# Softmax attention with bit-built exponentials: one of VectorE's three shifted copies is made by DMA instead

## The chip, the cores and the metric

One core of one Trainium2 chip. The metric is the device time of one execution in microseconds (us). Each kernel was run several times; the text quotes the median. An execution is called slow when it lies over 1.5% above the fastest of the same kernel; such executions are left out of every ratio, though not of the medians.

## The reference

Two independent attention layers over 2048 positions with 32 heads of 16 channels, whose outputs stand side by side.

```python
# A: softmax attention
scores = einsum("bhqd,bhkd->bhqk", q, k) * scale
p = softmax(scores)
o = einsum("bhqk,bhkd->bhqd", p, v)
a = o.reshape(B, S, D) @ wo
# B: linear attention with softmax features
phi_q = concat([softmax(q @ w_phi), softmax(-q @ w_phi)])     # phi_k likewise
kv = einsum("bhsf,bhsd->bhfd", phi_k, v); z = phi_k.sum(s)
b = ((phi_q @ kv) / (phi_q @ z + 1e-6)) @ wo
out = concat([a, b])                                           # along the channels
```

What matters is A: 32 x 2048 x 2048 exponentials. B is small and is woven in between.

## The kernel before

The work of A is cut into 32 units (four heads, 512 query positions) of 16 key tiles. A key tile is 128 keys; its exponentials for the four heads are 128 x 2048 numbers. Most key tiles go to ScalarE, which exponentiates scores out of the score buffers. For up to five of the 16 (`DK`) VectorE builds the exponential from its bits: the score times a constant plus a constant, written as a 16-bit integer, is the bit pattern of a 16-bit float near the exponential. To make the error small, the same bits are used four times, shifted by 0, 256, 512 and 768, and the four results are added by TensorE with weighted values (`VJ`). So a tile costs VectorE four evictions of scores (128 x 512 each, read out of the buffer into which TensorE wrote them) and three copies with an added constant (128 x 2048 each):

```python
# four evictions write the bits into rg[i]; the product with the values follows
firsts.append(put(dv_a, _Task("dve", 0.6, one("dve", cv), [qk], ...)))
put(pe_pd, pv_task(u, firsts + [v_ready[kt]], ..., lambda r: tile(q0.res["i"], r), ...))
for j in range(1, _NPH):                                       # _NPH = 4: three copies
    ad = put(dv_ad, _Task("dve", 0.59, one("dve", lambda e, t, j=j: e.tensor_scalar(
        rg[:, t.res["j"].idx, :], rg[:, q0.res["i"].idx, :], float(sh[j]), 32767.0, ALU.add, ALU.min)),
        firsts, lat=DL, need=[("j", rj_sl, 1, 1)], rel=[lambda: [q0.res["i"]]], port=True))
    put(pe_pd, pv_task(u, [ad, vj_ready[(kt, j)]], ..., lambda r, ad=ad: tile(ad.res["j"], r), ...))
# ... (cut)
```

`put` does not issue anything. A planner in the kernel's source gives each task a duration and a latency (`_Task(engine, us, ..., lat=...)`), simulates the engines, and fixes once the order in which each engine gets its instructions. On the chip every engine then works in that order and waits where a semaphore is not there yet. Whatever comes later than the planner assumed holds up all that stands behind it (in the change TensorE's matmuls wait so for an accumulate 32 times, 57.4 us in all).

## Time and profile before

| | before |
|---|---|
| median of 3 runs | 770.23 us (770.06 to 772.56) |
| span of the profiled run, granted clock | 767.3 us, 0.996 |
| ScalarE busy | 745.1 us, 97% |
| TensorE, VectorE, GpSimd busy | 714.4, 724.6, 149.8 us |
| DMA queues | 23.38 MB |
| wide exponentials' idle time ahead of them | 3.8 us |

Busy time is the sum of an engine's instructions. "Idle before" a group is time in which its engine did nothing until one of its instructions could start, with what ended most of it. The granted clock is TensorE's, as a share of full speed. The lines themselves stand in the prediction below.

### The profile page before, as it was taken

The page shows a single profiled execution, that of the slowest core. Times are in us where ns is not written, and L with a number is a line of the kernel's source. Part 1 is how long each engine was busy: PE and PEld are TensorE (multiplying, and loading weights), DVE is VectorE, ACT ScalarE, POOL GpSimd, SP SyncE. Part 2 cuts the span into 40 slices and gives each one's busy share as a digit, 9 for nine tenths or more (in the row PEclk, how much of TensorE's full clock was granted, in tenths as well). Part 3 has the DMA queues.
Part 4 walks back from the last instruction along what each step waited for, and adds up shares of the span by engine and source line. Part 5 has one row for each costly group of instructions (what it writes and reads, how often), then busy time and mean ns, then how long its engine had stood idle before and what let it go on. Part 6 is the DMA issues. An engine that isn't in the chain of part 4 may idle for free.

```text
span 767.3 us, 17162 instructions
## 1 busy us (share of the span) xinstructions
PE 714.4 (93%) x7122; PEld 217.4 (28%) x7209; DVE 724.6 (94%) x1315; ACT 745.1 (97%) x846; POOL 149.8 (20%) x218
## 2 busy tenths in 40 slices
PE   8999999999899998999899999999999999999996
PEld 3322222223222222232222223322222222222222
DVE  2799999999899999999999999999999999999996
ACT  6999999999899999999999999999999999999994
POOL 3321111110111131212121113222222113121120
PEclk9999999999999999999999999999999999999999
DMA  6200000018300110000000010000000001010002
GB/s 153 68 3 26 8 15 19 16 25 143 97 15 11 33 32 15 8 14 19 16 17 18 16 33 17 16 13 22 26 23 23 26 25 30 18 31 30 11 25 65
DMA packets 43871, 23.38 MB, mean 30 GB/s; under 512 B 31180, under 2 KB 39820, under 8 KB 43788
## 3 DMA queue, kind: packets, MB, share of 16 engines
q1 hardware_dynamic: 42204, 21.45, 10.4%
q8 instruction: 57, 0.93, 0.5%
q10 hardware_dynamic: 1584, 0.79, 0.4%
q14 instruction: 26, 0.21, 0.1%
HBM read 11.81 MB, written 4.45 MB: 21 GB/s over the span
## 4 chain that ended last, share of the span: by engine, by line
ACT 85%; PE 7%; DVE 4%; DMA 2%; issue 0%; SPq 0%; ACTq 0%
ACT pT L962 80%; PE PS L755 2%; DVE rg L1020 2%; PE PS L748 2%; ACT e_k L1172 2%; DMA sums<-X 2%; ACT eT L1235 1%; DVE rg L1031 1%; DMA OT<-in_A_x_dram 1%; ACT Wf L1235 1%; PE PS L877 0%; ACT KT L677 0%; ACT VP L657 0%; DVE Wf L1157 0%; PE PS L646 0%
## 5 line engine op out<-in xcount | busy, mean ns | idle before, releaser
L962 ACT ACTIVATE pT<-PS 128x1024 bf16<-128x1024 f32 (+1 forms) x755 | 706.9, 1093 | 4.0 <-PE PS L748 3.7
L1020 DVE TENSOR_SCALAR rg<-PS 128x512 uint16<-128x512 f32 x524 | 339.7, 682 | 10.5 <-PE PS L748 8.7
L748 PE MATMUL PS<-QT,KT 32*128 32x512 bf16 x2048 | 317.5, 385 | 20.7 <-ACT pT L962 13.8
L1031 DVE TENSOR_SCALAR rg<-rg 128x2048 uint16<-128x2048 uint16 x393 | 256.9, 689 | 0.7 <-PE PS L755 0.5
L748 PEld LDWEIGHTS PS<-QT,KT 32*128 32x128 bf16 x2048 | 80.5, 91 | 284.4 <-ACT pT L962 225.6
L755 PE MATMUL PS<-pT,VP 128*32 128x512 bf16 x1524 | 150.3, 389 | 4.1 <-ACT pT L962 2.0
L755 PE MATMUL PS<-rg,VJ 128*32 128x512 f16 x1572 | 144.0, 386 | 3.6 <-DVE rg L1031 3.1
L755 PEld LDWEIGHTS PS<-pT,VP 128*32 128x32 bf16 x1524 | 39.1, 94 | 82.6 <-issue 51.2
L1182 POOL TENSOR_TENSOR w<-e_k,stat 128x512 bf16<-128x512 bf16 x32 | 33.1, 1056 | 119.5 <-DVE stat L1178 67.3
L755 PEld LDWEIGHTS PS<-rg,VJ 128*32 128x32 bf16 x1572 | 38.3, 95 | 53.9 <-issue 22.3
L755 PE MATMUL PS<-rg,VP 128*32 128x512 f16 x524 | 51.9, 386 | 0.1
L1282 POOL TENSOR_TENSOR w<-w,den 128x256 bf16<-128x256 f32 x32 | 19.3, 619 | 113.4 <-DVE den L1278 70.3
L835 POOL TENSOR_TENSOR OT<-X,Yd 128x256 bf16<-128x256 f32 x30 | 21.7, 741 | 95.8 <-DMA Yd<-scr 78.2
L835 POOL TENSOR_TENSOR Oo<-X,Yd 128x256 bf16<-128x256 f32 x30 | 21.4, 733 | 81.5 <-DMA Yd<-scr 38.1
L649 PE MATMUL PS<-xT,w 128*128 128x512 bf16 x105 | 32.3, 382 | 3.9 <-issue 2.5
L1272 POOL TENSOR_TENSOR w<-w 128x272 f32<-128x272 f32 x32 | 23.7, 760 | 61.1 <-DVE rg L1031 42.8
L1258 DVE TENSOR_TENSOR w<-PS,stat 128x408 f32<-128x408 f32 (+1 forms) x48 | 25.2, 526 | 0.2
L803 DVE COPY X<-PS 128x512 f32<-128x512 f32 x32 | 21.9, 684 | 2.5 <-PE PS L755 2.5
L782 PE MATMUL PS<-ones_t,zer 128*32 128x512 bf16 x252 | 24.2, 388 | 0.0
L685 POOL TENSOR_SCALAR KT<-KT,hmask 128x512 bf16<-128x512 bf16 x12 | 8.3, 692 | 68.7 <-DVE KT L659 46.4
L1175 DVE TENSOR_REDUCE stat<-e_k 128x64 f32<-128x1024 bf16 x16 | 19.4, 1212 | 0.2
L755 PEld LDWEIGHTS PS<-rg,VP 128*32 128x32 bf16 x524 | 13.7, 95 | 19.2 <-issue 10.5
(103 smaller groups left out, 418.4 us busy)
## 6 DMA issues: line engine op xcount, KB each, us to landing
Yd<-scr SPq DMA_DIRECT2D x31, 256.0 KB
out_dram<-e_k SPq DMA_DIRECT2D x16, 128.0 KB, 1.7
out_dram<-OA SPq DMA_DIRECT2D x12, 128.0 KB, 1.7
OT<-Oo SPq DMA_DIRECT2D x60, 16.0 KB, 1.8
w<-in_A_wqkv_dram SPq DMA_DIRECT2D x2, 384.0 KB, 4.9
OT<-in_A_x_dram SPq DMA_DIRECT2D x1, 512.0 KB, 4.7
w<-in_A_wqkv_dram ACTq DMA_DIRECT2D x1, 512.0 KB, 6.4
WOp<-in_A_wo_dram SPq DMA_DIRECT2D x1, 512.0 KB, 6.0
```

Source lines behind the costliest of these rows:

```text
L649: return e.matmul(bank_of(t), w[:, ct, c0:c0 + 128], xT[:, ct, c * 512:(c + 1) * 512], start=(ct == 0), stop=(ct == 3))
L748: return e.matmul(out_ap, KT[32 * r:32 * r + n, g, kt * 128:(kt + 1) * 128], QT[32 * r:32 * r + n, c, g // 2, :], start=True, stop=True, t ...
L755: return e.matmul(PS[32 * r:32 * r + 32, pvb[u].idx, :], lhs(8 * (g // 2) + 2 * r + g % 2), rhs(r), start=t.res["first"], stop=t.res["last ...
L782: P.op("pe", lambda e, r=r: e.matmul(PS[32 * r:32 * r + 32, pvb[u].idx, :], zer[:], ones_t[:].unsqueeze(1).broadcast_to([128, 4, 128]), st ...
L803: xv = _Task("dve", 0.61, one("dve", lambda e, t: e.tensor_copy(X[:, t.res["x"].idx, :], PS[:, pvb[u].idx, :])), [], lat=DL, need=[("x", x ...
L835: ms.append(put(po_n, _Task("pool", 0.7, one("pool", lambda e, t, cs=cs: e.tensor_tensor(OT[:, c % 2, g // 2, cs] if even else Oo[:, ms[0] ...
L962: return e.activation(pT[:, p:p + n, :].rearrange("p a n -> p (a n)"), PS[:, b:b + n, :].rearrange("p a n -> p (a n)"), ACT.Exp, scale=0.25)
L1020: return e.tensor_scalar(rg[:, q0.res["i"].idx, 512 * r:512 * r + 512], PS[:, qk.res["D"].idx, :], ya, yb, ALU.mult, ALU.add)
L1031: ad = put(dv_ad, _Task("dve", 0.59, one("dve", lambda e, t, j=j: e.tensor_scalar(rg[:, t.res["j"].idx, :], rg[:, q0.res["i"].idx, :], flo ...
L1182: ph.append(put(po_phi, _Task("pool", 1.03, one("pool", lambda e, t, a=a: e.tensor_tensor(pk[ph[0].res["k"].idx][:, 512 * a:512 * a + 512] ...
L1258: muls.append(put(dv_y, _Task("dve", 0.485, one("dve", lambda e, t, yv=yv, lo=lo, n=n: e.tensor_tensor(ysv[r0.res["y"].idx][:, 136 * lo:13 ...
L1272: ad = [put(po_y, _Task("pool", 0.73, one("pool", lambda e, t, k=k: e.tensor_tensor(y3(0)[:, 2 * k:2 * k + 2], y3(0)[:, 2 * k:2 * k + 2], ...
```

## The change

The intent is to take work from VectorE, so that it can build more tiles and ScalarE fewer. The first of the three shifted copies is made by two transfers: a constant from DRAM is copied into the buffer (512 KB, issued from SyncE), then GpSimd issues a DMA that adds the bits onto it.

```diff
-    NPT = 15
-    NB, NJ = 2, 4
-    NR = NB + NJ
+    NPT = 13
+    NB, NJ, ND = 3, 2, 3            # buffers: bits, VectorE's copies, DMA's copies
+    NR = NB + NJ + ND
...
-        for j in range(1, _NPH):
+        pf = put(sp_pf, _Task("sp", 0.5, dma(..., lambda e, t, i: e.dma_start(
+            rg[:, t.res["j"].idx, :], sh_d[:].broadcast_to([128, 2048]))), [l_sh], lat=3.3, need=[("j", rd_sl, 1, 1)]))
+        ac = put(po_a, _Task("pool", 1.1, sw(..., lambda e, t: e.dma_start(
+            rg[:, pf.res["j"].idx, :], rg[:, q0.res["i"].idx, :], accum_op=ALU.add)), [pf] + firsts, lat=5.0,
+            rel=[lambda: [q0.res["i"]]]))
+        put(pe_pd, pv_task(u, [ac, vj_ready[(kt, 1)]], ..., lambda r: tile(pf.res["j"], r), ...))
+        for j in range(2, _NPH):
             ad = put(dv_ad, ...
...
-    Oo = sb("Oo", [128, 2, 512], BF)
+    Oo = sb("Oo", [128, 1, 512], BF)
-    OA = sb("OA", [128, 2, 512], BF)
+    OA = sb("OA", [128, 1, 512], BF)
```

Cut from it: a new table of the planner's weights; a start with smaller transposes and a first projection by quarters; key maskings and half of a reduction moved to GpSimd; an ending in which 16 output products stand ahead of the last unit's sum and that sum is copied in halves; sorted final waits; loads of weights moved from ScalarE's queue to SyncE's, and another buffer (`eT`) halved. The planner's two figures: it assumes 3.3 us for the constant and 5.0 us for the accumulate.

## The prediction

> **What bounds the kernel now.** I read the page's busy row first, then the chain of work that ended last, then the groups by shape, and last a table of stretches.
>
> ```profile
> PE 714.4 (93%) x7122; PEld 217.4 (28%) x7209; DVE 724.6 (94%) x1315; ACT 745.1 (97%) x846; POOL 149.8 (20%) x218
> ...
> ACT 85%; PE 7%; DVE 4%; DMA 2%; issue 0%; SPq 0%; ACTq 0%
> ```
>
> Three engines are above 90%, so the busy row alone does not name a bound. The chain does: 85% of it is ScalarE, and four fifths of the span is one line, the exponentials. VectorE, the engine that the change relieves, has 4% of it.
>
> ```profile
> L962 ACT ACTIVATE pT<-PS 128x1024 bf16<-128x1024 f32 x741 | 690.1, 1086 | 3.8 <-PE PS L748 3.5
> L1020 DVE TENSOR_SCALAR rg<-PS 128x512 uint16<-128x512 f32 x524 | 339.7, 682 | 10.5 <-PE PS L748 8.7
> L1031 DVE TENSOR_SCALAR rg<-rg 128x2048 uint16<-128x2048 uint16 x393 | 256.9, 689 | 0.7 <-PE PS L755 0.5
> L962 ACT ACTIVATE pT<-PS 128x1536 bf16<-128x1536 f32 x14 | 21.0, 1503 | 0.2 <-PE PS L748 0.2
> ```
>
> The wide exponentials lost 3.8 us to waiting before them in the whole run. The 393 copies of L1031 are the three shifts of each of 131 VectorE tiles (524 evictions, four to a tile). Their mean of 689 ns is not their cost: they start about 0.6 us apart (the chain shows them at 0.60), so the group takes 257 us rather than 271. The exponentials likewise: 48 in a row in the chain took 44.00 us, 0.917 us each.
>
> ```profile
> 0.00:10.18 10.18, 7.71 (x44) 3.51 (x44) 2.46 (x4) 3.40 (x5) 4.16 (x15) 1.00 0.82 204
> ...
> 40.00:183.00 143.00, 138.20 (x1298) 38.36 (x1309) 141.81 (x246) 143.00 (x155) 18.31 (x26) 1.00 0.10 22
> 183.00:203.00 20.00, 17.28 (x177) 5.64 (x173) 16.88 (x30) 16.71 (x18) 1.00 (x1) 0.91 0.78 169
> ...
> 289.00:640.00 351.00, 327.52 (x3477) 101.64 (x3518) 343.03 (x632) 351.00 (x404) 75.83 (x104) 1.00 0.06 20
> ...
> 755.00:768.00 13.00, 5.92 (x27) 2.72 (x25) 6.02 (x22) 2.64 (x7) 0.00 (x0) 0.89 0.19 57
> ```
>
> Columns: stretch, length, busy time of PE, weight loads, VectorE, ScalarE, GpSimd, granted clock, DMA share, GB/s. From 40 to 183 and from 289 to 640 ScalarE is busy for every microsecond. It idles in three places: the start (first exponential at 10.18), the end (after the last exponential at 754.3), and 3.3 us in 183 to 203, where the loads of the second half hold the DMA engines at 0.78. So the time is ScalarE's work plus those gaps. A faster VectorE shortens nothing by itself; it helps only if ScalarE is given fewer tiles or if a gap shrinks.
>
> [...] its 512 KB loads land in 4.3 to 4.7 us, though among other loads. [...] The copies here do 2048 elements in 689 ns, about 3 a nanosecond, against 0.75 for an eviction (512 in 682 ns)[...].
>
> **The change part by part.** Counts are from the built order of instructions of both kernels.
>
> 1. VectorE's tiles go from 131 to 136 (524 to 544 evictions), its copies from 393 to 272. At 0.6 us, 121 copies fewer take away 73 us and 20 evictions more add 12. The key reduction over 1024 elements (1212 ns, 16 times) becomes a sum of halves on GpSimd and a smaller reduction, perhaps 0.6 us less each, 10 us in all. Twelve key maskings leave for GpSimd, and some evictions come over from ScalarE. VectorE falls by 65 to 70 us, to some 655. None of this is on the chain.
>
> 2. ScalarE, the part that counts. Exponentials go from 741 of two pieces and 14 of three to 716 and 24. A two-piece one takes 0.917; a three-piece one I put at 1503 - (1086 - 917) = 1334 ns. Before: 741 x 0.917 + 14 x 1.334 = 698.2. After: 716 x 0.917 + 24 x 1.334 = 688.6. That is 9.6 us less. Four value evictions (0.49) and three key evictions (about 0.62) fewer are 3.8 us more. ScalarE's work between first and last exponential falls by 13.4 us. This is the main gain, and note how small it is beside 73 us: only five tiles change engine.
>
> 3. TensorE: the five tiles need 3 x 5 x 4 = 60 extra value matmuls, at four in parallel and about 0.216 us, 3 us[...]. It stays at about 714 of a shorter span, some 95%.
>
> 4. GpSimd: [...]32 additions of halves (perhaps 0.7 us), 12 maskings: 30 us of counted work, some 180 in all.
>
> 5. DMA: per tile 512 KB of a constant and 512 KB accumulated. 136 x 1 MB is about 143 MB against 23.38 MB now; the DMA row should go from 10% to half or more.
>
> 6. Start: smaller transposes and a projection by quarters. Chaining the measured pieces (input landed 5.6; transpose 0.3, copy 0.4, four in a pipeline to 7.4; last projection 7.9; eviction 8.7; scores and exponential) I put the first exponential at 9.3 instead of 10.18: 0.9 us.
>
> 7. End: before, 754.83 to 760.41 passes between the last sum's copy and the first output eviction, 3.45 of it 16 output matmuls in a row. Those move ahead of the last sum, which is copied in halves; the final waits are sorted. I take 2.5 us.
>
> Sum without new waits: 770.2 - 13.4 - 0.9 - 2.5 = 753.4.
>
> **The wait that could take the gain back.** TensorE runs in order, so a late accumulated copy stops it, and ScalarE, with two score buffers, soon after. From the built program I counted the exponentials whose scores TensorE issues between a tile's last score matmul and the matmul that waits for its accumulated copy. The median is 9 exponentials, 9 x 0.917 = 8.3 us; the lowest tenth is 7, 6.4 us. Into it must fit matmul (0.4), eviction with a turn in the queue (0.7 to 1.3), GpSimd's issue[...], and the accumulate. [...] So some tiles of the 136 should be late by a fraction of a microsecond to one. As accumulates overlap, I charge 2 us, and 2 us more for the load burst, where 0.78 of the DMA engines is already taken. That gives 757.
>
> **The rivals.**
>
> A. *Late copies become the bound.* If an accumulate takes 7 to 8 us in company, the chain is late at nearly every tile. One microsecond at 136 tiles, with one and a half in flight, is about 90 us. For it: three buffers only, a tile each 5.5 us, each buffer held through constant, accumulate and matmul; the small sums<-X transfer took 4.77 us in the burst. Against: the order was laid out anew, with more distance than the old copies needed. Outcome 785 or more.
>
> B. *The offload relieves an idle resource.* VectorE is not on the chain, and if ScalarE's reduction is eaten by DMA contention in the burst and by the 95% TensorE, only start and end remain: 762 to 768.
>
> C. *Everything is hidden*, and VectorE's slack also removes the small waits of 4 to 5 us in the middle. Then 749 to 752.
>
> D. *TensorE becomes the bound*: the 93% rises to 95%, and each ordering loss goes to the end. It would look like B.
>
> **Range and chances.** The sum without waits lies at 753.4, the 2% line at 770.23 x 0.98 = 754.8. The waits I charge put the middle past that line, and their tail goes one way. Range 748 to 773. Faster by over 2%: 0.38; within 2%: 0.53; slower by over 2%: 0.09, which is rival A.
>
> **What would show it.** Right: ScalarE still over 95% busy and over 80% of the chain, the wide exponentials near 690 us in all, VectorE near 87%, DMA share over half, and waits of TensorE for the accumulated tile under 5 us. Wrong: a row in the waits in which value matmuls wait for the DMA with tens of microseconds, or exponentials with idle time before them well over 4 us (A); ScalarE's idle grown just in 183 to 203 or beside TensorE at 97% (B, D); first exponential not before 9.5, or more than 11 us from last exponential to end, would void parts 6 and 7.

## More of the kernel before

At the end of each unit a chain of small transfers (8 KB for `sums`, 8 KB for `scr`, 256 KB for `Yd`) makes the divisor of the softmax:

```python
d1 = put(sp_q, ... e.dma_start(sums[:, 16 * u:16 * u + 16], X[16 - g % 2:128:32, xi, :]))    # 16 numbers a row
rc = put(dv_n, ... e.reciprocal(rin[...], sums[:, 16 * u:16 * u + 16]), [d1])                # VectorE
d2 = put(sp_q, ... e.dma_start(scr[u]..., rin[...]), [rc])                                   # to DRAM
d3 = put(sp_q, ... e.dma_start(Yd[...], scr[u].unsqueeze(1).broadcast_to([4, 32, 512])), [d2])
ms.append(put(po_n, ... e.tensor_tensor(OT[...], X[...], Yd[...], ALU.mult), [d3]))          # GpSimd
# ... (cut)
```

One more view of this kernel matters later, its longest waits for small transfers: engine and line, then total us, times, longest.

```profile
POOL OT L835 <- DMA Yd<-scr: 78.2, 10, 20.4
...
POOL Oo L835 <- DMA Yd<-scr: 38.1, 7, 10.7
...
DVE rin L817 <- DMA sums<-X: 3.7, 3, 2.4
```

GpSimd stands 116.3 us waiting for `Yd`, and nothing comes of it: nothing urgent is behind it in its queue.

## The result, and the profile after

| | before | after |
|---|---|---|
| median | 770.39 us | 944.2 us (932.78 to 947.09, 4 runs) |
| span of the profiled run, clock | 767.3, 0.996 | 942.8, 0.869 |
| ScalarE busy | 745.1 | 749.9 |
| VectorE, TensorE, GpSimd busy | 724.6, 714.4, 149.8 | 690.0, 788.4, 312.7 |
| DMA | 23.38 MB | 166.05 MB |

The ratio is 1.220 (95% interval 1.209 to 1.231). Ratios here are the mean time of one kernel's fast runs over that of the other's of the same rounds, so they are not quite the ratio of the medians quoted.

The page of the kernel after: busy row, clock and DMA by slices of a fortieth of the span (tenths), the chain of work that ended last.

```profile
PE 788.4 (84%) x7172; PEld 220.1 (23%) x7251; DVE 690.0 (73%) x1214; ACT 749.9 (80%) x821; POOL 312.7 (33%) x399
...
PEclk9997899889798979778969989799987896799699
DMA  6777787879776856877767887877664885869563
...
DMA 37%; PE 28%; DVE 16%; issue 6%; ACT 6%; POOL 3%; SPq 3%; POOLq 0%; DVEq 0%
DMA rg<-rg 17%; PE PS L778 12%; PE PS L771 10%; DVE rg L1061 7%; DMA sums<-X 7%; ACT pT L1003 6%; DMA Yd<-scr 5%; DVE rg L1079 4%; DMA scr<-rin 4%; SPq L596 2%; DMA out_dram<-OA 2%; DMA rg<-sh_d 2%; POOL OT L869 1%; DVE X L831 1%; PE PS L1249 1%
```

No engine is above 84%: where the time went is waiting, not work. The chain has turned over. Before, ScalarE held 85% of it; now it has 6%, and transfers have 37%: the accumulate (`rg<-rg`) 17%, and the three small transfers together 16% (sums 7, Yd 5, scr 4). The clock row is the second surprise: before, the stretches in the prediction show 1.00 nearly everywhere; now 19 of the 40 slices are below nine tenths.

The groups, and the landing of the two new transfers:

```profile
L1003 ACT ACTIVATE pT<-PS 128x1024 bf16<-128x1024 f32 (+1 forms) x740 | 715.0, 1064 | 174.0 <-PE PS L771 171.1
L1061 DVE TENSOR_SCALAR rg<-PS 128x512 uint16<-128x512 f32 x544 | 355.6, 681 | 104.9 <-PE PS L771 102.3
...
L1073 POOL DMA_DIRECT2D rg<-rg x136 | 125.3, 922 | 371.2 <-DVE rg L1061 180.7
L778 PE MATMUL PS<-rg,VJ 128*32 128x512 f16 x1632 | 168.4, 439 | 61.6 <-DMA rg<-rg 57.4
L1079 DVE TENSOR_SCALAR rg<-rg 128x2048 uint16<-128x2048 uint16 x272 | 194.2, 736 | 16.5 <-PE PS L778 15.4
...
rg<-sh_d SPq DMA_DIRECT2D x136, 512.0 KB, 5.6
rg<-rg POOLq DMA_DIRECT2D x136, 512.0 KB, 6.0
```

The exponentials' idle time went from 4.0 us (3.8 for the wide ones alone) to 174.0 us; that is nearly the whole difference. They wait for scores (`PS L771`), that is, for TensorE. Stretches of the kernel after (start and end, length, busy time of PE, weight loads, VectorE, ScalarE and GpSimd with counts, clock, DMA share, GB/s), to set beside the same stretches in the prediction:

```profile
40.00:183.00 143.00, 119.73 (x1066) 30.59 (x1081) 111.44 (x181) 118.13 (x121) 47.69 (x60) 0.91 0.77 179
183.00:203.00 20.00, 17.08 (x140) 4.10 (x142) 14.92 (x25) 16.17 (x17) 4.83 (x7) 0.83 0.85 206
289.00:640.00 351.00, 294.11 (x2943) 80.83 (x2964) 267.90 (x457) 286.02 (x322) 123.82 (x147) 0.86 0.75 179
```

The loss is spread evenly: from 289 to 640 ScalarE is busy 286.02 of 351 us, where it was busy for all of them. It is not a matter of the burst of loads, nor of the ends.

What the engines stand waiting for:

```profile
ACT pT L1003 <- PE PS L771: 171.1, 150, 6.2
...
PEld PS L778 <- DMA rg<-rg: 70.2, 39, 3.8
POOL OT L869 <- DMA Yd<-scr: 68.0, 12, 10.0
PE PS L778 <- DMA rg<-rg: 57.4, 32, 3.4
POOL Oo L869 <- DMA Yd<-scr: 56.1, 15, 7.9
POOL rg L1073 <- DMA rg<-sh_d: 40.4, 14, 7.0
DVE rin L847 <- DMA sums<-X: 35.7, 13, 6.2
```

TensorE's matmuls waited for the accumulate 32 times, 57.4 us, 1.8 us each. VectorE's wait for sums went from 3.7 to 35.7. GpSimd's wait for `Yd` is about what it was, 124.1 against 116.3; but the queue in which it stands now also holds the accumulates.

One such moment, as a timeline (start, us, engine, line, operation; in brackets the idle time before it and what ended it):

```profile
410.09 0.72 POOL L869 TENSOR_TENSOR OT<-X,Yd 128x256 bf16<-128x256 f32 x1 [1.71 <-DMA Yd<-scr]
...
411.25 0.88 POOL L1073 DMA_DIRECT2D rg<-rg  x1 [0.44 <-DMA rg<-sh_d]
...
412.26 3.19 DVE L1079 TENSOR_SCALAR rg<-rg 128x2048 uint16<-128x2048 uint16 x1
412.54 2.35 POOL L1240 TENSOR_TENSOR w<-e_k,stat 128x512 bf16<-128x512 bf16 x2
414.53 0.62 PE L778 MATMUL PS<-rg,VJ 128*32 128x512 f16 x4 [2.93 <-DMA rg<-rg]
...
416.69 2.11 ACT L1003 ACTIVATE pT<-PS 128x1024 bf16<-128x1024 f32 x2 [3.70 <-PE PS L771]
...
424.35 0.40 PE L778 MATMUL PS<-pT,VP 128*32 128x512 bf16 x4
```

Read it in order. GpSimd stands 1.71 us for `Yd` and then 0.44 us for a constant before it issues an accumulate. TensorE stands 2.93 us for an accumulate. When it goes on, four value matmuls take 0.62 us instead of 0.40: the clock records have half clock from 413.2, 1.6 us after the stop began, for 10.2 us, three times 3.413 us. ScalarE lost 3.70 us at the stop, and goes on starving: from 412 to 424 it was busy 6.40 of 12 us. At 424.35 the group takes 0.40 again. One more thing in passing: VectorE's copy at 412.26, whose like take 0.69 us, took 3.19 while GpSimd multiplied beside it. Why it did, no run isolated, but it is small: the 272 copies took 736 ns each on average here and 724 in the first experiment below, against 689 in the kernel before; that is 13 us in all here, and 10 in the first experiment, which was only 6 us slower than the kernel before.

In the whole run TensorE spent 246 us at half clock, in 33 stretches, of which 32 last a whole number of times 3.413 us (the last is cut by the end); before it was 5.5 us in two. Of ScalarE's 193 us without work (942.8 - 749.9), 109 lie in those stretches. Half clock follows here after a single stop of 1.62 us (four value matmuls before, and after the change of the clock at 505.4):

```profile
503.95 0.40 PE L778 MATMUL PS<-rg,VJ 128*32 128x512 f16 x4 [1.62 <-DMA rg<-rg]
...
505.30 0.59 PE L778 MATMUL PS<-rg,VJ 128*32 128x512 f16 x4
```

Worked out from the records of this trace (from 20 us on, without the end): all half-clock stretches start on one fixed grid of 3.413 us. A window of that grid at full clock in which TensorE stood idle for 1.6 us or more in sum was followed by half clock in 22 of 22 cases, one with under 1.0 us in none of 154, and one between in 9 of 18. So stops shorter than a window were enough here. These are counts of one trace; no run isolates what sets the clock.

Granted clock and half clock are one number in two forms, since only full and half occur in these records: half-clock time = 2 x (1 - clock) x span, here 2 x 0.131 x 942.8 = 247 us (the clock is rounded). The table of the experiments uses it.

### The profile page after: what moved, and what is told of

It reads as the page before. It is cut to its first block, busy times and chain, and to the rows that moved or that the text cites. A ratio compares the mean times of both kernels' runs of the same rounds, so it can differ in the third digit from the quotient of the medians.

```text
span 942.8 us, 17573 instructions
## 1 busy us (share of the span) xinstructions
PE 788.4 (84%) x7172; PEld 220.1 (23%) x7251; DVE 690.0 (73%) x1214; ACT 749.9 (80%) x821; POOL 312.7 (33%) x399
## 2 busy tenths in 40 slices
DMA packets 83045, 166.05 MB, mean 176 GB/s; under 512 B 35533, under 2 KB 44173, under 8 KB 82958
## 3 DMA queue, kind: packets, MB, share of 16 engines
HBM read 83.12 MB, written 4.45 MB: 93 GB/s over the span
## 4 chain that ended last, share of the span: by engine, by line
DMA 37%; PE 28%; DVE 16%; issue 6%; ACT 6%; POOL 3%; SPq 3%; POOLq 0%; DVEq 0%
DMA rg<-rg 17%; PE PS L778 12%; PE PS L771 10%; DVE rg L1061 7%; DMA sums<-X 7%; ACT pT L1003 6%; DMA Yd<-scr 5%; DVE rg L1079 4%; DMA scr<-rin 4%; SPq L596 2%; DMA out_dram<-OA 2%; DMA rg<-sh_d 2%; POOL OT L869 1%; DVE X L831 1%; PE PS L1249 1%
## 5 line engine op out<-in xcount | busy, mean ns | idle before, releaser
L1003 ACT ACTIVATE pT<-PS 128x1024 bf16<-128x1024 f32 (+1 forms) x740 | 715.0, 1064 | 174.0 <-PE PS L771 171.1
L1061 DVE TENSOR_SCALAR rg<-PS 128x512 uint16<-128x512 f32 x544 | 355.6, 681 | 104.9 <-PE PS L771 102.3
L771 PE MATMUL PS<-QT,KT 32*128 32x512 bf16 x2048 | 337.5, 427 | 43.8 <-DMA rg<-rg 11.6
L1073 POOL DMA_DIRECT2D rg<-rg x136 | 125.3, 922 | 371.2 <-DVE rg L1061 180.7
L778 PE MATMUL PS<-rg,VJ 128*32 128x512 f16 x1632 | 168.4, 439 | 61.6 <-DMA rg<-rg 57.4
L1079 DVE TENSOR_SCALAR rg<-rg 128x2048 uint16<-128x2048 uint16 x272 | 194.2, 736 | 16.5 <-PE PS L778 15.4
L778 PE MATMUL PS<-pT,VP 128*32 128x512 bf16 x1504 | 163.8, 432 | 5.1 <-ACT pT L1003 2.2
L771 PEld LDWEIGHTS PS<-QT,KT 32*128 32x128 bf16 x2048 | 78.6, 92 | 351.1 <-ACT pT L1003 171.7
L778 PE MATMUL PS<-rg,VP 128*32 128x512 f16 x544 | 59.8, 430 | 0.3 <-DVE rg L1061 0.3
L831 DVE COPY X<-PS 128x512 f32<-128x512 f32 (+1 forms) x33 | 22.0, 670 | 26.5 <-PE PS L778 18.6
L847 DVE RECIPROCAL rin<-sums 128x16 f32<-128x16 f32 x31 | 7.7, 248 | 35.9 <-DMA sums<-X 35.7
L1231 POOL TENSOR_TENSOR w<-e_k 128x256 f32<-128x256 bf16 x32 | 22.8, 770 | 14.9 <-PE PS L1260 8.1
```

Source lines behind the costliest of these rows:

```text
L771: return e.matmul(out_ap, KT[32 * r:32 * r + n, g, kt * 128:(kt + 1) * 128], QT[32 * r:32 * r + n, c, g // 2, :], start=True, stop=True, t ...
L778: return e.matmul(PS[32 * r:32 * r + 32, pvb[u].idx, :], lhs(8 * (g // 2) + 2 * r + g % 2), rhs(r), start=t.res["first"], stop=t.res["last ...
L831: xvs.append(_Task("dve", 0.34 if last else 0.61, one("dve", lambda e, t, k=k: e.tensor_copy(X[:, xvs[0].res["x"].idx, n * k:n * k + n], P ...
L1003: return e.activation(pT[:, p:p + n, :].rearrange("p a n -> p (a n)"), PS[:, b:b + n, :].rearrange("p a n -> p (a n)"), ACT.Exp, scale=0.25)
L1061: return e.tensor_scalar(rg[:, q0.res["i"].idx, 512 * r:512 * r + 512], PS[:, qk.res["D"].idx, :], ya, yb, ALU.mult, ALU.add)
L1073: ac = put(po_a, _Task("pool", 1.1, sw(lambda t: d_ac[pf.res["j"].idx - NB - NJ], lambda e, t: e.dma_start(rg[:, pf.res["j"].idx, :], rg[: ...
```

## The experiments

Two theories at first. *L*: TensorE, in order, stands for late accumulates, and the clock makes it worse. *S*: the new traffic delays the small transfers, behind which VectorE, SyncE and GpSimd stand in order. All ran on the same order of instructions as the change unless said otherwise.

### The order of the change without its traffic

Both transfers cut to 16 of 128 partitions; the buffers are filled once at the start, by VectorE. Wrong on purpose. What is left of the transfers is an eighth: 41.27 MB in all, and a DMA share of 0.33 from 40 to 180 us, where it was 0.09 before.

```diff
-            rg[:, j, :], sh_d[:].broadcast_to([128, 2048])
+            rg[0:16, j, :], sh_d[:].broadcast_to([16, 2048])
-            rg[:, j, :], rg[:, i, :], accum_op=ALU.add
+            rg[0:16, j, :], rg[0:16, i, :], accum_op=ALU.add
```

> The changed kernel with its instruction order kept, but both transfers of a tile cut from 128 partitions to 16 (64 KB in place of 512 KB each). The result is wrong on purpose: most of the second copy's rows keep a constant. All waits, all 136 issues from GpSimd and the whole plan stay; only the bytes go. Theory L (the landing of large transfers in company is later than the order of TensorE allows for): 750 to 762 us, granted clock above 0.98, exponentials idle under 15 us. Theory G (GpSimd's issuing[...]) and theory R (the new order, the smaller buffers, the work moved to GpSimd): still above 850 us, clock under 0.92.

Measured 779.12 us (777.37 to 781.96), ratio 1.0078 (1.0056 to 1.010), half clock 41 us, exponentials' idle time 25.6 us. So the transfers' size is worth 944.2 - 779.1 = 165 us; GpSimd's 136 issues and the new order, theories G and R of the expectation, are not the main cause, as they stay. The expectation of 750 to 762 was missed all the same. What the run lies above before (772.88 in the same rounds, 6 us) is in part this edit's own: the fill takes VectorE 5.18 us from 4.45 on, and the first exponential begins at 14.33 us, where it began at 10.31 in the change. The rest, some 2 us, is the order with what is left of the transfers; and the 165 us, like every distance from 779.1 below in a run without the fill, would be some 4 us more, by this one profile. Stretches of this run, then two of before:

```profile
40.00:180.00 140.00, 137.30 (x1320) 36.45 (x1316) 132.12 (x218) 139.70 (x148) 53.81 (x71) 1.00 0.33 43
180.00:240.00 60.00, 51.30 (x518) 15.20 (x510) 39.98 (x66) 49.04 (x50) 12.68 (x17) 0.89 0.57 99
240.00:600.00 360.00, 340.20 (x3668) 101.65 (x3666) 333.20 (x596) 354.83 (x411) 159.21 (x195) 0.99 0.32 43
600.00:700.00 100.00, 94.48 (x880) 26.29 (x878) 88.24 (x166) 93.65 (x105) 33.50 (x49) 0.93 0.33 50
```

```profile
180.00:240.00 60.00, 55.75 (x576) 16.50 (x571) 56.67 (x96) 56.71 (x62) 6.73 (x8) 0.97 0.31 71
...
600.00:700.00 100.00, 93.83 (x926) 27.97 (x940) 99.10 (x189) 99.95 (x113) 19.41 (x31) 1.00 0.08 26
```

ScalarE's work is 734.3 us against 745.1: the gain that was the aim is there. In the even part, 40 to 180, ScalarE is as full as before (139.70 of 140). But the order idles elsewhere: 11.0 us in the loads of the second half (180 to 240), against 3.3 before; 6.4 from 600 to 700, against 0.1; 5.2 from 240 to 600.

### One transfer at a time

The accumulate cut to 16 partitions and the constant whole (wrong); then the constant cut and, in place of the accumulate, a plain copy of the same 512 KB from the same queue. The plain copy leaves unshifted bits where shifted ones belong; the tolerance let that pass as correct.

```diff
# accumulate small
+            rg[0:16, j, :], rg[0:16, i, :], accum_op=ALU.add
# plain copy
-            rg[:, j, :], rg[:, i, :], accum_op=ALU.add
+            rg[:, j, :], rg[:, i, :]
```

> As the run before, but only the accumulate is cut to 16 partitions; the constant is copied in full. Wrong result on purpose. If the accumulate itself is what is late (L, narrow): 755 to 775 us, since the constant is fetched a whole buffer turn ahead. If any heavy traffic is enough, because it delays the small transfers (sums, reciprocals) on which GpSimd and VectorE wait in order (theory S): 800 to 880.

> The constant cut to 16 partitions and the accumulate replaced by a plain copy of the same 512 KB from GpSimd[...]. Wrong result on purpose (the copy is not shifted). L: landing median near 4 us, time 755 to 790. S: half the traffic is left, 800 to 860. G: above 850.

Measured 791.3 us (1.0243) and 794.67 us (1.0287): the constant's traffic alone costs 12 us over 779.1, a plain copy alone 16. Landing: the constant 4.4 us at the median with no company but the small accumulate, the plain copy 3.2. Both lie between the ranges of the two theories. Either of these two alone is nearly harmless.

### The change without its copy

All of the change (start, ending, moved work, planner's weights) but three copies on VectorE and the buffers `NB, NJ, ND = 3, 5, 0`.

```diff
-        pf = put(sp_pf, ...); ac = put(po_a, ...); put(pe_pd, pv_task(u, [ac, ...
-        for j in range(2, _NPH):
+        for j in range(1, _NPH):
```

> The whole change except the DMA copy: all three shifted copies on VectorE again, with 3 buffers for bits and 5 for copies; the scheduler lays the order out anew with the change's weights, which were not tuned for this. Right result. L, S and G: 755 to 780 us, clock above 0.98. R: above 850.

Measured 782.69 us (777.85 to 789.27), ratio 1.0160 (1.011 to 1.0211), correct, just over the 780 expected at most; half clock 12 us, exponentials' idle time 13.7. So there is no hidden gain elsewhere that the copy spoils: the rest of the change does not beat the kernel before either.

### Both copies, and the add by itself

The whole change with a plain copy in place of the add; then the add alone: constant small, 512 KB accumulated from a tile of zeros (wrong; a weight tile was dropped to make room).

```diff
# plain copy beside the constant
-            rg[:, j, :], rg[:, i, :], accum_op=ALU.add
+            rg[:, j, :], rg[:, i, :]
# add alone
+            rg[:, j, :], zt[:], accum_op=ALU.add        # zt: zeros; constant cut to 16 partitions
```

> The changed kernel with the same transfers of 512 KB twice a tile, but the one from GpSimd copies in place of accumulating[...] (the copied bits are not shifted). Full traffic of writes stays. If the bytes written and the company of the two transfers are what is late: landing of the copy near 5 us, over 880 us. [...] landing under 4.5 us and 795 to 830 us.

> The accumulate in full (128 partitions, 512 KB, from a tile of zeros, so that the numbers stay finite), the constant cut to 16 partitions; wrong result on purpose. To make room for the zeros, the output weights of the second half are loaded to DRAM in place of SBUF. If the accumulate alone is too slow for the distance planned: landing 5.5 us or more and over 850 us. If only both together are (theory L in company): landing 4.5 to 5 us, 790 to 830 us.

Measured 826.83 us (818.3 and 835.36; the second and profiled run was a slow one, no ratio) and 875.43 us (1.1343). The add alone costs 96 us over 779.1, where the plain copy alone cost 16. The line of landings (KB each, median us from issue to landing) in this run, and the plain copy's in the run with the constant cut:

```profile
rg<-zt POOLq DMA_DIRECT2D x136, 512.0 KB, 5.2
```

```profile
rg<-rg POOLq DMA_DIRECT2D x136, 512.0 KB, 3.2
```

Adding takes 2.0 us longer to land for the same bytes, with issue at 0.88 us of GpSimd's time against 0.58. The two copies together cost 48 (39 by the one fast run), less than the add alone: the add is what makes the transfers heavy, and company then makes it worse still (165). The landings lie between what was expected of them: 5.2 us for the add alone, and 3.8 for the plain copy beside the constant.

### Telling the planner the truth

Only latencies in the source, which change the order; all results correct. First the two transfers' measured medians, roughly, then late landings, then late small transfers with the large ones as in the change, then the second plan with both transfers cut small (wrong).

```diff
-  pf: lat=3.3      ac: lat=5.0
+  pf: lat=5.6      ac: lat=6.5          # medians
+  pf: lat=7.0      ac: lat=9.0          # late
-  sums: 2.6   scr: 2.2   Yd: 2.6
+  sums: 4.8   scr: 3.5   Yd: 6.5        # small transfers later
```

> The changed kernel in full, right result, with the scheduler told other landings: 5.6 us for the constant (was 3.3) and 6.5 for the accumulate (was 5.0). It then places the matmuls that read the sum later and gives VectorE fewer tiles. L: the late waits fall by half or more, 820 to 880 us, clock above 0.92. If the order of TensorE does not matter and the transfers cost by themselves: still above 920.

> As the run before with 7.0 and 9.0 us, near the longest landings seen (10.4 and 11.0). L: hardly a wait for the accumulate left, 775 to 830 us, clock above 0.96, though fewer tiles go to VectorE and ScalarE has more work. If the transfers cost by themselves: still above 920.

> The changed kernel in full, right result, the two large transfers planned as before (3.3 and 5.0 us), but the scheduler told that the small ones of a unit's end take longer: 4.8 us for the sums (was 2.6), 3.5 for their reciprocals' write (was 2.2), 6.5 for the spread back (was 2.6). Theory S (VectorE and GpSimd stand in order behind small transfers that the traffic delays, and so issue the accumulate late): 850 to 900 us. Theory L (the accumulate itself): within 20 us of 944.

> The order of the run that planned 7.0 and 9.0 us (879 us), with both large transfers cut to 16 partitions. It splits that run's loss. If the order itself, starved because three buffers are held longer, costs it: 830 us or more. If the traffic costs it, through the small transfers: 780 to 800 us. Wrong result on purpose.

Measured 918.8 (1.1905), 879.48 (1.1395), 904.69 (1.1702) and 826.41 us (1.069). A plan for the medians wins little, 25 us. The late plan removes TensorE's waits for the accumulate (0 to 2 us left), but it buys them with VectorE's tiles: 117 instead of 136, ScalarE's work up to 775.4 us. Its order costs 826.4 - 779.1 = 47 us even without traffic, and the traffic still adds 53. Planning the small transfers later alone wins 40 us, a first sign that they matter as much as the large ones, though this plan also has 130 accumulates and not 136. None of the four times lies in an expected range (904.69 and 826.41 miss one by 5 and 4 us): neither theory alone foretold them.

### A part of the tiles

The DMA copy for two of the five key tiles of a unit (57 accumulates instead of 136), VectorE for the others.

```diff
+        by_dma = kt in (3, 12)
-    NB, NJ, ND = 3, 2, 3
+    NB, NJ, ND = 3, 3, 2
```

> Only two of a unit's five key tiles take the DMA copy (57 accumulates in place of 136; two buffers for them, three for VectorE's copies), right result. If a late accumulate costs about the same each time, 57/136 of the loss of some 160 us over all copies on VectorE: 783 + 67 = 850. If the loss grows with company, as between the single transfers (12 and 97 us) and both (165): 790 to 815. Below 772, better than the kernel before, only if the offload pays at all: I expect not.

Measured 823.99 us (816.48 and 831.49, no ratio), correct: 41 over 782.69 with 42% of the accumulates, where all of them cost 161 (944.2 - 782.7). It lies between the two expectations (815 and 850). A quarter of the loss for four tenths of the transfers: the loss grows faster than their number. At neither number is there a gain. (The orders of the three differ, and of this run's two executions one was slow; by the fast one, 816.5, it is 33 of 157.)

### Before with the new ending

The kernel before, with the change's new ending alone (cut to its core; the sorted final waits came with it):

```diff
-        bcs = [put(pe_op, ... PS[..., 256 * k:256 * k + 256], sel[:], X[:, xi, 256 * k:256 * k + 256] ..., [xv], ...
+        bcs = [put(pe_ls, ..., [xvs[0]], ...), put(pe_ls, ..., [xvs[1]], ...)]   # the last sum copied in halves
+    def last_firsts(c):                                # 16 output products ahead of that sum
+        for st in (1, 0, 2, 3):
+            for p in range(4): fours.append(put(pe_op, ... [mul[8 * c + (1, 3, 5, 6)[p]], ...
```

> The kernel before with the change's ending alone: the last sum copied in halves, the sixteen output products ahead of it, the range check of the earlier sums earlier, the final waits sorted. Right result, no DMA copy, the same order up to the end. The last exponential to the end took 13.0 us before and 10.4 in the run with small transfers: 1.5 to 2.6 us faster than the kernel before, 769 to 771 on a chip where that takes 772.

Measured 775.75 us, ratio 1.0013 (0.9987 to 1.0039): the same; the gain expected did not come. In its profile the 16 output products did not run ahead: the multiplication they need came late.

```profile
764.47 0.68 DVE L844 TENSOR_TENSOR OT<-X,Yd 128x512 bf16<-128x512 f32 x1
...
765.21 0.39 PE L907 MATMUL PS<-WOl,OT 128*128 128x512 bf16 x1 [2.29 <-DVE OT L844]
...
769.21 0.63 PE L907 MATMUL PS<-WOl,OT 128*128 128x512 bf16 x1
```

TensorE stood 2.29 us for it and ended at half clock (0.63 us; the granted clock is 0.87 over 755 to 775). The new ending is worth something only where that multiplication is early, so this run does not value it for the change's own order.

### Taking away each wait, with all the traffic

These set L against S. Every engine's instructions, in kind and order, are those of the change (but for a fill or two at the start), and every transfer is still issued; only what makes one engine wait is replaced. Their outputs are wrong, which doesn't matter for the times.

```diff
# accumulate's wait: its value matmuls read a constant tile
-            lambda r: tile(pf.res["j"], r)
+            lambda r: ones_t[:].unsqueeze(1).broadcast_to([128, 4, 128])
# small transfers' waits
-            e.reciprocal(rin, sums[...])             # waits for sums
+            e.reciprocal(rin, rk[:])                 # a constant
-            Yd <- scr[u], after scr                  # waits for scr
+            Yd <- A_x[0][0:8, :]                     # an input, as large
-            OT = X * Yd                              # waits for Yd
+            OT = X * X
```

> The whole change with all its traffic and the same order of every engine, but the matmuls of the accumulated copy read a constant tile of ones and do not wait for the accumulate (wrong result on purpose; a tile's buffer still waits for its accumulate before the next constant comes in). Theory L (TensorE stands in its in-order queue waiting for the accumulate[...], which is most of the loss): 790 to 840 us, clock 0.95 or more, the exponentials' idle time under 50. Theory S (the delayed small transfers sums, scr and Yd, behind which VectorE and GpSimd stand in order, are most of the loss): still above 890, clock below 0.91. Both matter about equally: 840 to 890.

> The whole change with all its traffic and the same order, the accumulate waited for as before, but no engine waits for the small transfers any more: the reciprocal reads a constant tile, GpSimd multiplies X by itself, and the broadcast into Yd comes from an input (wrong result on purpose; every transfer is still issued). L: still 900 to 945. S: 790 to 860. An earlier run in which only the plan was told of later small transfers gave 904.69, so if that was the same effect in another form, about 900.

> Both waits taken away, all traffic left. If L and S together are the whole loss: 775 to 800, near the 779 of the same order without the two large copies. If the traffic also slows the engines themselves or something third stands in the way ([...]buffers held by late copies, late outputs): 810 or more.

Measured 904.23 us (1.1685), 872.09 us (no ratio) and 819.86 us (1.0652). My theory L fell: without any wait for the accumulate in a value matmul 40 of the 165 us go, far less than I had expected of it. The small transfers' waits are worth 72, which neither theory had: the time lies between the two ranges. Together they are worth 124, a little more than 40 + 72, and 41 remain. (Half of the runs without the small waits were slow; by the fast runs the small waits are worth 75, the accumulate's 38, both 122.) Where they remain, in the list of waits of the run with both taken away:

```profile
POOL rg L1082 <- DMA rg<-sh_d: 74.4, 21, 7.4
...
ACT pT L1012 <- PE PS L777: 56.4, 59, 6.7
PE PS L777 <- DMA rg<-rg: 25.4, 18, 6.0
```

Score matmuls now wait for the accumulate (18 times, 25.4 us; 11.6 in the change): a buffer of evicted bits is not free while a late accumulate still reads it. And GpSimd stands for the constant, 74.4 us.

### Which queue, and which buffer

Of the small transfers' waits only GpSimd's taken away; then the run with both waits away, in which the accumulate adds a tile of zeros and so holds no buffer of bits.

```diff
# GpSimd only
+            OT = X * X                               # reciprocal and Yd as in the change
# no buffer held
-            rg[:, j, :], rg[:, i, :], accum_op=ALU.add
+            rg[:, j, :], zt[:], accum_op=ALU.add
```

> Of the small transfers' waits only GpSimd's is taken away: its multiplications read X in place of Yd and do not wait for Yd (wrong result on purpose); VectorE still waits for sums, and every transfer and the order are as in the change. Theory H (GpSimd stands in its in-order queue for a late Yd, and the accumulate behind it in that queue is issued late, so TensorE waits longer): most of the 72 us that removing all small waits gave, so 870 to 895. Theory V (VectorE waiting for sums, with the evictions and copies behind it, is most of it): 910 to 940.

> As the run with both waits taken away (819.86 us), and the accumulate now adds a constant zero tile in place of the evicted bits, so that no buffer of evicted bits is held by a late accumulate and no score matmul waits for one (wrong result on purpose; sizes, order and issue moments as before). If the buffers are what is left of the loss: 780 to 800, and no wait of the scores for the accumulate. If the traffic itself or GpSimd's wait for the constant holds things up: 805 to 820.

Measured 906.46 us (1.1746) and 805.61 us (1.0421). The first lies between both expectations: 38 of the 72 us come through GpSimd, 34 through the other two queues (VectorE's for sums, SyncE's for scr; these two runs do not part them). By the fast runs it is 36 and 39: about half each. How GpSimd's part works can be read from the times of its instructions. From the end of a tile's fourth eviction to the start of its accumulate's issue, over the 136 tiles (evictions in fours and accumulates paired in order), worked out from the trace: in the change 0.98 us at the median and 4.5 at the ninth decile; with GpSimd's wait away 0.61 and 2.8; in the order without traffic 0.57 and 2.4. The accumulates were issued late because GpSimd stood for `Yd`.

The second came out at the edge of what I had expected of the traffic: the buffers account for 14 us of the remaining 41. The last 26 over 779.1 are open. In this run's profile, a slow one, no score matmul waits for the accumulate any more, and GpSimd still stands 127.7 us for the constant; no run takes that wait away.

| run | us | fast runs, mean | half clock, us | over 779.1 |
|---|---|---|---|---|
| order without traffic | 779.1 | 779.4 | 41 | 0 |
| no waits, no buffer held | 805.6 | 804.7 | (slow run) | 26 |
| no waits | 819.9 | 818.3 | 63 | 41 |
| no small waits | 872.1 | 865.0 | 107 | 93 |
| no wait for the accumulate | 904.2 | 902.4 | (slow run) | 125 |
| no GpSimd wait | 906.5 | 904.2 | 187 | 127 |
| the change | 944.2 | 940.4 | 247 | 165 |

The half clock falls with the loss. I did not find an edit that holds the clock up and leaves the waits, so how much of each step is the wait itself and how much the clock after it stays open. No run beat the kernel before; it remains the best.

## Why the prediction was wrong

It said 757 us, range 748 to 773, with 0.09 for slower by over 2%. The outcome is rival A's "785 or more".

**The step that failed** is the last term of the sum, in "The wait that could take the gain back": "some tiles of the 136 should be late by a fraction of a microsecond to one. As accumulates overlap, I charge 2 us". In its place the runs show some 165 us for the traffic of these copies. How long the accumulate takes to land was the author's estimate in it, which no trace had shown; the measured median was 6.0 us. Four things in it were wrong.

- It set one median (8.3 us of distance) against a sum of typical parts. What counts is the tail: the accumulate lands in 4.5 to 11.0 us, and its issue starts 0.98 us after the last eviction at the median but 4.5 at the ninth decile. I had allowed for GpSimd's issue, but for no queueing ahead of it.
- It took the measured loads of 512 KB as 4.3 to 4.7 us. The trace before has five: 4.3, 4.7, 5.2, 6.0 and 6.4. With the last for the accumulate, the matmul (0.4), the eviction (1.3) and an issue of 0.92 us as measured since, the sum is 9.0, over the median distance before anything is charged for the adding. (Alone, adding cost 2.0 us over a plain copy: 5.2 against 3.2.)
- It looked at one wait. The same traffic made the small transfers late, which I had not charged at all, and these waits cost more (72 us) than the accumulate's own (40). They couple: a late `Yd` holds GpSimd, which issues the next accumulate late (GpSimd's waits are 38 of the 72 us).
- It charged a wait with its length. TensorE stood 57.4 us for the accumulate in 32 waits; half clock can follow such a stop, as at 413.2 (10.2 us); it took 246 us of this run in all, and 109 of ScalarE's 193 idle us lie in those stretches.

**Rival A** named the right outcome for half of the right reason. It wanted landings of 7 to 8 us; the median was 6.0. It charged only the accumulate, though it named a slow `sums` transfer as a sign; the accumulate's wait alone is worth 40 us, not 90.

**Part 1** (VectorE falls by 65 to 70, to some 655): it fell to 690.0. The copies cost more than the 0.6 us at which they follow each other in a full stream; 272 took 194.2, or 0.71 each. That cost nothing.

**Part 2** (ScalarE's work falls by 13.4): right in kind. In the order without traffic it fell by 10.8 us; in the change the busy time is 749.9, because an exponential that starts after a wait overlaps none before it (1.02 us alone, 0.917 in a row; by the 150 waits an estimate of 15 us).

**Part 3** (TensorE stays at about 714): 788.4, as its matmuls are longer at half clock (0.62 us for four instead of 0.40 in the timeline); 730.8 without the traffic.

**Parts 4 and 5**: GpSimd 312.7 instead of some 180 counted, because the page counts the issue of an accumulate (136 at 0.92 us, 125.3 us), which is not in that sum. DMA 166.05 MB, as 23 + 143; its share well over half, as said.

**Part 6** (first exponential at 9.3): missed in the change's profile, where it began at 10.31, before at 10.18. But in five other runs of the same order, in which VectorE fills nothing at the start either, it began between 8.89 and 9.89, so one profile does not decide this part.

**Part 7** (end 2.5 us shorter): from the last exponential to the end 13.0 us before, 12.7 in the change, 10.4 in the order without traffic and 11.5 with the copies on VectorE, but 13.7 with the plain copy alone. It came in some runs and not in others, and what decides is open.

**The burst** ("2 us more for the load burst") is mis-sized too: from 180 to 240 ScalarE idled 11.0 us even with an eighth of the traffic, against 3.3.

So without the copies' traffic the sum would have been 755 (757 less the 2 us for late copies) and measured 779. In that run's profile ScalarE's work between the first and the last exponential fell by 9.9 us, but its idle time there grew by 21.3 (from 5.1 to 26.4), and the fill at the start took 4. Even without the fill, in this order, the change would not have won 2%.

## What to carry to other kernels

Before moving work from an engine that is not on the chain to DMA, list every queue in which an instruction will wait for a transfer, with what stands behind it. Here the new traffic delayed the small old transfers too (median landing of `scr` from 1.4 to 3.2 us, of a 128 KB output from 1.7 to 3.8; VectorE's wait for `sums` from 3.7 to 35.7 us in all), and a delay spread through a queue in order: GpSimd's waits for `Yd`, ahead of the accumulates' issues, cost 38 us. Compare distances with the late end of a transfer's landings, not with its median (the accumulate's: 11.0 against 6.0 us), and look up what TensorE's granted clock does after short stops (here half clock followed a single stop of 1.62 us). A wait that cost nothing (GpSimd's 116 us for `Yd`) becomes expensive the day an urgent issue is put behind it in the same queue.
